# Spills by 128 partitions, tap blocks shifted by matmuls, token tiles moved by eight, weights loaded by GpSimd, and a new order, in the backward kernel of a speech encoder block

## The chip, the cores and the metric

One core of a Trainium2 chip runs the whole program. Its engines are TensorE (PE, with its weight loads as PEld), VectorE (DVE), ScalarE (ACT), GpSimd (POOL) and SyncE (SP); DMAs are issued by SP, ACT and GpSimd. The metric is the device time of one execution in microseconds, the median over runs. Lower is better.

## The reference

The block is an E-Branchformer layer: x is layer-normalized, one branch is global attention over all 4000 tokens, the other a local branch with a five-tap depthwise convolution as a gate; both are concatenated, passed through a five-tap depthwise convolution (dw_merge), projected by w_merge, and added to x. The kernel returns the output and, for a given grad_out, the gradients of all eight inputs. B = 2, T = 4000, D = 144, K = 5, bf16.

```
xa  = layernorm(x)
q, k, v = split(xa @ w_qkv)
attn = softmax(q @ k^T * D**-0.5) @ v
glob = attn @ w_att_out
h   = gelu(layernorm(x) @ w_mlp_in);  u, g = split(h);  g = layernorm(g)
gc[t] = sum_i gpad[t + i] * dw_csgu[i]              # i = 0..4
loc = (u * gc) @ w_mlp_out
m   = concat(glob, loc)
mc[t] = sum_i mpad[t + i] * dw_merge[i]
out = x + (m + mc) @ w_merge
out, vjp = jax.vjp(block, x, 7 weights)
return out, *vjp(grad_out)
```

## The kernel before

Tokens lie in tiles of 125 partitions (PB) by 32 blocks (NB) per batch, so a tensor of a batch is 125 x 32 x 144. A copy of 125 partitions is made in two DMAs, by `move` and `load_tok`: rows 0 to 111, and the 13 rows from 112.

The program has three stages that overlap at their ends.

*Head* (to about 50 us): x is loaded and normalized (xa_aug), transposed by TensorE, and the weights are loaded (`Head.loads`), transposed and multiplied into fused matrices. `Head.vu` makes, for each half h of the merge, the product VU of taps and weights, and a small block VUs of five taps by 16 rows (the last 16 of the 144 channels): GpSimd multiplies it into the tile sr (128 x 2 x 80), TensorE multiplies sr by w_merge, ACT casts the result, and it is spilled to VUs_d. What the tail needs is that block at four row offsets of 16, so the tail clears two tiles and loads VUs_d four times each, at shifted rows (lines 1632 to 1635).

*Attention* (`phase_att`): 64 steps, one for each block of 125 queries of both batches. A step computes scores S by TensorE (lines 1187 and 1194), the row minimum by DVE (L1209), the exponent by ACT (L1215), which is Pbuf, its transpose PT by two DMA transposes (L1219), and Y = P times xa by TensorE (L1236). For the gradient it computes dP the same way, multiplies it by P (ACT L1225, DVE L1226: Sbuf), transposes that by DMA (L1405: ST), multiplies it by xa (Z, L1266), and adds up the gradient of xa over the keys (X, L1322, added to acc by DVE, L1329). Beside the steps the local branch runs in units of two blocks (steps 2 to 27 for batch 0, 34 to 61 for batch 1). It goes forward and backward over a ring of neighbours, and where a batch's units go round, the last unit's tiles hgr, dugr and gpr are kept in DRAM (`keep`, stored in `e_m`, loaded by `e_hold`), as is a part of the ring (`held`). The tensors xa of batch 0 (xa_d, eight parts) and acc of batch 0 (acc_d, four parts) are spilled to DRAM in the loop and loaded again in the tail (load_xa0, load_acc0).

*Tail* (from about 1026 us): out is computed by `out_g` (TensorE L1708 and L1710, with x added by DVE, L1711), x is loaded by `load_x` in groups of four blocks, each in two DMAs, and out is stored in the same groups; dx, the weight gradients and the final products follow.

The order of instructions on each engine is written out in the code: the class `Planner` has a table `ORDER`, one list of numbers for each of PE, DVE, Activation, Pool and SP, and `plan` ties each engine's runs of instructions into that order. An engine takes its instructions in this order alone, so an instruction that waits holds back all that stand behind it on its engine, and SP's list is the order in which nearly all DMAs are issued, the transposes of PT (L1219), ST (L1405), qt (L1165) and dhT (L691) among them.

## Time and profile before

| | us |
|---|---|
| median of 3 runs | 1149.53 (1149.24 to 1152.27) |
| profiled execution | 1152.39 |
| its span on the core | 1150.5 |
| PE busy | 1118.8 (97%) |
| DVE busy | 1021.0 (89%) |
| ACT busy | 906.5 (79%) |
| POOL busy | 249.5 (22%) |

The granted clock of TensorE is 0.999 in mean. A row of a view reads "line engine operation out<-in"; SPq and POOLq are the queues on which SP and GpSimd issue DMAs, and an instruction DMA_DIRECT2D there is the issue of one DMA. The time of such an issue is that of the issuing engine; when the data have landed is another number. A row of waits reads: engine, line, what it waited for, total us, times, longest.

### The profile page before, as it was taken

The page shows a single profiled execution, that of the slowest core. Times are in us where ns is not written, and L with a number is a line of the kernel's source. Part 1 is how long each engine was busy: PE and PEld are TensorE (multiplying, and loading weights), DVE is VectorE, ACT ScalarE, POOL GpSimd, SP SyncE. Part 2 cuts the span into 40 slices and gives each one's busy share as a digit, 9 for nine tenths or more (in the row PEclk, how much of TensorE's full clock was granted, in tenths as well). Part 3 has the DMA queues.
Part 4 walks back from the last instruction along what each step waited for, and adds up shares of the span by engine and source line. Part 5 has one row for each costly group of instructions (what it writes and reads, how often), then busy time and mean ns, then how long its engine had stood idle before and what let it go on. Part 6 is the DMA issues. An engine that isn't in the chain of part 4 may idle for free.

```text
span 1150.5 us, 35851 instructions
## 1 busy us (share of the span) xinstructions
PE 1118.8 (97%) x14293; PEld 868.7 (76%) x14293; DVE 1021.0 (89%) x3063; ACT 906.5 (79%) x1641; POOL 249.5 (22%) x427
## 2 busy tenths in 40 slices
PE   6999999999999999999999999999999999999998
PEld 3667777777777677777777777777777777699987
DVE  8699999999999998877999999999999997667656
ACT  5999898899898767777989889888889877615372
POOL 8111112111121113431001111111111112013642
PEclk9999999999999999999999999999999999999999
DMA  4688887979988989998988989888888899978973
GB/s 117 155 160 176 173 181 158 192 159 173 174 166 159 188 181 182 201 187 183 207 183 178 171 158 168 161 181 152 173 174 154 187 177 183 224 173 219 245 144 101
DMA packets 680887, 200.72 MB, mean 174 GB/s; under 512 B 657815, under 2 KB 674093, under 8 KB 680699
## 3 DMA queue, kind: packets, MB, share of 16 engines
q1 hardware_dynamic: 678352, 194.69, 84.6%
q0 software_dynamic: 2192, 3.62, 1.1%
q8 instruction: 111, 1.82, 0.7%
q14 instruction: 56, 0.46, 0.1%
q10 hardware_dynamic: 176, 0.12, 0.0%
HBM read 24.62 MB, written 18.01 MB: 37 GB/s over the span
## 4 chain that ended last, share of the span: by engine, by line
PE 64%; DMA 13%; DVE 11%; ACT 7%; issue 2%; SPq 1%; POOL 1%; ACTq 0%; DVEq 0%; POOLq 0%
PE X L1322 18%; PE ps L1187 14%; PE yz L1236 8%; PE yz L1266 8%; PE ps L1194 5%; DMA PT<-Pbuf 5%; DVE Pbuf L1209 4%; ACT Pbuf L1215 3%; PE po L1708 2%; DMA ST<-Sbuf 2%; PE pd L610 1%; DVE Sbuf L1226 1%; PE pj L1147 1%; ACT Sbuf L1225 1%; DMA go_h<-in_grad_out_dram 1%
## 5 line engine op out<-in xcount | busy, mean ns | idle before, releaser
L1209 DVE TENSOR_SCALAR_CACHE_REDUCE Pbuf<-ps 125x1000 bf16<-125x1000 f32 x256 | 306.2, 1197 | 30.1 <-PE ps L1194 22.4
L1225 ACT CAST Sbuf<-ps 125x1000 bf16<-125x1000 f32 x249 | 248.7, 999 | 86.7 <-PE ps L1194 66.2
L1215 ACT ACTIVATE Pbuf<-Pbuf,nm 125x1000 bf16<-125x1000 bf16 x256 | 284.9, 1144 | 4.4 <-DVE nm L1211 4.2
L1322 PE MATMUL X<-QBs,Pbuf 125*128 125x144 bf16 x2048 | 281.1, 226 | 0.2 <-POOL QBs L1256 0.2
L1322 PE MATMUL X<-QBs,Sbuf 125*128 125x144 bf16 x2048 | 281.3, 226 | 0.0
L1187 PE MATMUL ps<-xaT_m,qt 128*128 128x500 bf16 x1024 | 260.6, 374 | 5.0 <-DVE Pbuf L1209 3.5
L1322 PEld LDWEIGHTS <-Sbuf 125*128 125x128 bf16 x2048 | 198.2, 98 | 18.8 <-issue 18.5
L1322 PEld LDWEIGHTS <-Pbuf 125*128 125x128 bf16 x2048 | 200.2, 98 | 1.3 <-issue 1.1
L1226 DVE TENSOR_TENSOR Sbuf<-Sbuf,Pbuf 125x1024 bf16<-125x1024 bf16 x249 | 170.8, 690 | 7.9 <-ACT Sbuf L1225 6.0
L1236 PE MATMUL yz<-xa_aug,PT 125*128 125x145 bf16 x2048 | 151.0, 227 | 6.5 <-DMA PT<-Pbuf 6.4
L1266 PE MATMUL yz<-xa_aug,ST 125*128 125x144 bf16 x2048 | 150.8, 228 | 3.6 <-DMA ST<-Sbuf 2.4
L1236 PEld LDWEIGHTS <-PT 125*128 125x128 bf16 x2048 | 130.7, 98 | 21.6 <-DMA PT<-Pbuf 10.5
L1187 PEld LDWEIGHTS <-qt 128*128 128x128 bf16 x1024 | 91.4, 97 | 68.6 <-issue 7.0
L1266 PEld LDWEIGHTS <-ST 125*128 125x128 bf16 x2048 | 132.9, 98 | 12.2 <-issue 7.1
L1329 DVE TENSOR_TENSOR acc<-X,acc 125x432 f32<-125x432 f32 (+1 forms) x204 | 109.8, 548 | 15.3 <-PE X L1322 14.8
L1256 POOL TENSOR_TENSOR QBs<-g,g 125x144 bf16<-125x144 f32 x64 | 35.2, 550 | 379.2 <-ACT g L1255 290.9
L1194 PEld LDWEIGHTS <-qt 16*128 16x128 bf16 x1024 | 26.3, 91 | 108.9 <-issue 108.9
L1194 PE MATMUL ps<-XR,qt 16*128 16x500 bf16 x1016 | 100.4, 380 | 0.0
L681 POOL TENSOR_SCALAR l_w<-ring,nc,c 125x144 f32<-125x144 bf16 x64 | 31.8, 504 | 167.0 <-DVE nc L677 122.4
L653 DVE TENSOR_TENSOR l_prod<-ring,Wc 125x720 bf16<-125x720 bf16 x128 | 65.9, 535 | 0.2
L1611 PE MATMUL Hps<-Yg,go_h 125*128 125x144 bf16 x640 | 54.3, 226 | 0.0
L600 POOL TENSOR_TENSOR rsr<-ve,mhalf 125x2 f32<-125x2 f32 x32 | 25.4, 795 | 126.9 <-DVE ve L599 107.4
(540 smaller groups left out, 1946.4 us busy)
## 6 DMA issues: line engine op xcount, KB each, us to landing
Yn_d<-yn SPq DMA_DIRECT2D x64, 36.0 KB
Zn_d<-qb SPq DMA_DIRECT2D x64, 36.0 KB
ug_d<-ugr SPq DMA_DIRECT2D x32, 72.0 KB
Yg<-Yn_d SPq DMA_DIRECT2D x8, 288.0 KB
Yg<-ug_d SPq DMA_DIRECT2D x8, 288.0 KB
Zn<-Zn_d SPq DMA_DIRECT2D x4, 576.0 KB
PT<-Pbuf SPq DMA_TRANSPOSE x128
ST<-Sbuf SPq DMA_TRANSPOSE x128
```

The lines of the kernel that those rows point to most:

```text
L653: nc.vector.tensor_tensor(prod[:, bi].rearrange("p a b -> p (a b)"), ring[:, a, p + bi:p + bi + 5, :].rearrange("p a b -> p (a b)"), W.Wc[ ...
L1187: mm = nc.tensor.matmul(pp[r // 2][:, r % 2, 0:CH], QT[i][:, 2 * h, :], bs(i)[0].xaT_m[:, c * CH:(c + 1) * CH], start=True, stop=False)
L1194: nc.tensor.matmul(pp[r // 2][:, r % 2, 0:CH], QT[i][rs, 2 * h + 1, :], xr, start=False, stop=True)
L1209: nc.vector.tensor_scalar(pv(pc(i, c2)), src, -1.0, 3.0e38, op0=ALU.mult, op1=ALU.min, accum_out=NM[i][:, c2:c2 + 1])
L1215: nc.scalar.activation(v, v, ACT.Exp, bias=NM[i][:, 4:5], scale=-1.0)
L1225: nc.scalar.copy(pv(sc(i, c2)), src)
L1226: nc.vector.tensor_tensor(sc(i, c2), sc(i, c2), pc(i, c2), op=ALU.mult)
L1236: nc.tensor.matmul(Yw, PT[0:PB, pos(i, j), :], S.xa_aug[:, j, 0:D + 1], start=(j == 0), stop=(j == NB - 1))
L1266: nc.tensor.matmul(Zw, ST[0:PB, j, :], S.xa_aug[:, j, 0:D], start=(j == 0), stop=(j == NB - 1))
L1322: nc.tensor.matmul(X[:, jj, :], l, r, start=(n_ == 0), stop=(n_ == len(ops) - 1))
L1329: nc.vector.tensor_tensor(av, X[0:PB, 0:nj, :], av, op=ALU.add)
L1611: nc.tensor.matmul(H[0:rows, a // 3, (a % 3) * D:(a % 3 + 1) * D], lhs, self.src[b][h][:, 2 + j, :], start=(n == 0 and a % 3 == 0), stop=( ...
```

## The change

Five parts.

1. *Weights.* Twelve loads of `Head.loads` (dw_merge, one; each half of w_merge, and w_att_out and w_mlp_out, two each; w_mlp_in, three) are issued by GpSimd and no longer by SP. w_qkv stays with ACT.
2. *Tap blocks.* sr becomes the middle of a tile of 176 columns that GpSimd clears. TensorE multiplies four windows of it by w_merge (8 matmuls of 128 x 144 for each h, before 2 of 80 x 144), ACT casts two tiles of 128 x 288 for each h (before one of 80 x 144), and VUs_d holds the four shifted blocks. The tail loads each in one DMA and clears nothing.
3. *Spills.* keep, xa_d and acc_d have 128 partitions and are moved in one DMA each. The tiles have 128 partitions too; their last rows are cleared by GpSimd (hgr, dugr, gpr, acc; acc is 4608 columns wide) or by two DMAs of SP from a zeroed tensor (xa).
4. *Tail.* `load_x` loads eight blocks at a time, and `out_g` stores eight at a time, but for the last two groups of batch 1.
5. *Order.* All five lists of `ORDER` are new. SP issues 750 DMAs and transposes in place of 826, GpSimd's list has 442 instead of 423 runs of instructions, PE's 1387 instead of 1385, ACT's 1644 instead of 1642, and DVE's as many as before.

The diff, with the lists cut to one line each of two engines:

```diff
         ld(self.Wqkv, k.w_qkv, 0)
-        ld(self.Wo, k.w_att_out, 0, nc.sync)
-        nc.sync.dma_start(self.dwt[:], k.dw_merge)
-        ld(self.Wl, k.w_mlp_out, 0, nc.sync)
-        for h in range(2):
-            ld(self.Wm[h], k.w_merge, h * D, nc.sync)
-        nc.sync.dma_start(W.Wi[0:128, 0, :], k.w_mlp_in[0:128, :])
-        nc.sync.dma_start(W.Wi[96:96 + DR, 1, :], k.w_mlp_in[128:D, :])
-        nc.sync.dma_start(self.Wi2[:], k.w_mlp_in[128:D, :])
+        e = nc.gpsimd
+        e.dma_start(self.dwt[:], k.dw_merge)
+        for h in (1, 0):
+            ld(self.Wm[h], k.w_merge, h * D, e)
+        ld(self.Wo, k.w_att_out, 0, e)
+        ld(self.Wl, k.w_mlp_out, 0, e)
+        e.dma_start(W.Wi[0:128, 0, :], k.w_mlp_in[0:128, :])
+        e.dma_start(W.Wi[96:96 + DR, 1, :], k.w_mlp_in[128:D, :])
+        e.dma_start(self.Wi2[:], k.w_mlp_in[128:D, :])
...
         W.VU.append(spill(k, v, "VU_d%d" % h))
-        sr = wt.tile([128, 2, 80], BF, name="sr%d" % h)
+        sw = wt.tile([128, 2, 176], BF, name="sr%d" % h)
+        nc.gpsimd.memset(sw[:], 0.0)
+        sr = sw[:, :, 48:128]
         for ch in range(2):
...
-        vs = wt.tile([80, D], BF, name="VUs%d" % h)
-        pt = self.ps([128, D], F32)
-        for ch in range(2):
-            nc.tensor.matmul(pt[0:80, :], sr[:, ch, :], self.Wm[h][:, ch, :], start=(ch == 0), stop=(ch == 1))
-        nc.scalar.copy(vs[:], pt[0:80, :])
+        vs = wt.tile([128, 4, D], BF, name="VUs%d" % h)
+        for q in range(2):
+            pt = self.ps([128, 2, D], F32)
+            for p in range(2):
+                a = 48 - DR * (2 * q + p)
+                for ch in range(2):
+                    nc.tensor.matmul(pt[:, p, :], sw[:, ch, a:a + 128], self.Wm[h][:, ch, :], start=(ch == 0), stop=(ch == 1))
+            nc.scalar.copy(vs[:, 2 * q:2 * q + 2, :], pt[:])
         W.VUs.append(spill(k, vs, "VUs_d%d" % h))
...
     nc.gpsimd.dma_start(held[1][PB - 1:PB].rearrange("p a b c -> p (a b c)"), k.zdram[0:1, 0:4 * D])
-    keep = [tc.dram_tile([PB, G2, n], BF, name="keep%d_%d" % (b, i)) for i, n in enumerate((D, D, 2 * D))]
+    keep = [tc.dram_tile([128, G2, n], BF, name="keep%d_%d" % (b, i)) for i, n in enumerate((D, D, 2 * D))]
     prod = pl.tile([PB, G2, 5, D], BF, name="l_prod")
...
         nc.gpsimd.memset(t[96:128], 0.0)
-    hgr = mk("hgr", [PB, G2, 2 * D], 3)
-    dugr = mk("dugr", [PB, G2, D], 3)
-    gpr = mk("gpr", [PB, G2, 2 * D], 3)
+    def whole(name, n):
+        full = mk(name, [128, G2, n], 3)
+        nc.gpsimd.memset(full[2][96:128], 0.0)
+        return full, [t[0:PB] for t in full]
+    hgf, hgr = whole("hgr", 2 * D)
+    dugf, dugr = whole("dugr", D)
+    gpf, gpr = whole("gpr", 2 * D)
     rsr = mk("rsr", [PB, 2 * G2], 4, F32)
...
     def e_hold():
...
             move(nc.sync, ring[:, :, 8 + 2 * i:10 + 2 * i, :], held[i])
-        move(nc.sync, hgr[0][:, :, 0:D], keep[0][:])
-        move(nc.sync, dugr[0][:], keep[1][:])
-        move(nc.sync, gpr[0][:], keep[2][:])
+        nc.sync.dma_start(hgf[0][:, :, 0:D], keep[0][:])
+        nc.sync.dma_start(dugf[0][:], keep[1][:])
+        nc.sync.dma_start(gpf[0][:], keep[2][:])
...
     def e_m(g):
...
         if g == NG2 - 1:
-            move(nc.sync, keep[0][:], hgr[new(g)][:, :, 0:D])
-            move(nc.sync, keep[1][:], dugr[new(g)][:])
-            move(nc.sync, keep[2][:], gpr[new(g)][:])
+            nc.sync.dma_start(keep[0][:], hgf[new(g)][:, :, 0:D])
+            nc.sync.dma_start(keep[1][:], dugf[new(g)][:])
+            nc.sync.dma_start(keep[2][:], gpf[new(g)][:])
...
 class Planner:
...
-        "Pool": [8, 5, 15, 4, 11, 0, 12, 10, 1, 3, 47, 7, 2, 16, 18, 6, 19, 17, 41, 25, 26, 24, 50, 33, 32, 31, 9, 53, 37, 38, 20, 30, 42, 23, 13,
...
-        "SP": [0, 1, 4, 3, 19, 2, 30, 5, 6, 9, 16, 21, 44, 10, 7, 45, 13, 18, 27, 39, 22, 46, 40, 60, 14, 12, 15, 23, 11, 8, 25, 31, 26, 28, 32, 20,
...
+        "Pool": [0, 22, 27, 7, 4, 2, 14, 1, 10, 9, 8, 20, 28, 19, 31, 30, 11, 6, 23, 29, 53, 37, 38, 36, 13, 44, 43, 45, 49, 12, 50, 32, 21, 15, 39,
...
+        "SP": [0, 1, 3, 2, 5, 4, 18, 48, 27, 13, 11, 6, 7, 30, 34, 29, 9, 15, 49, 10, 19, 20, 8, 21, 22, 24, 23, 26, 17, 14, 16, 12, 25, 35, 42, 31,
...
     def __init__(self, tc, nc):
...
         for h in range(2):
-            k.nc.gpsimd.memset(self.VUs[h][:], 0.0)
-            for a in range(4):
-                k.nc.sync.dma_start(self.VUs[h][DR * a:DR * a + 80, a, :], self.W.VUs[h][:])
+            k.nc.sync.dma_start(self.VUs[h][:], self.W.VUs[h][:])
...
         S = self.SS[0]
-        S.acc = m0.tile([PB, NB, D], F32, name="acc0")
-        S.xa_aug = m0.tile([PB, NB, XW], BF, name="xa0r")
+        self.acc0, self.xa0 = m0.tile([128, NB, D], F32, name="acc0"), m0.tile([128, NB, XW], BF, name="xa0r")
+        S.acc, S.xa_aug = self.acc0[0:PB], self.xa0[0:PB]
...
     def load_xa0(self):
...
             sl = slice(16 * g, 16 * g + 16)
-            move(k.nc.sync, S.xa_aug[:, sl, 0:D], k.xa_d[:, sl, :])
+            k.nc.sync.dma_start(self.xa0[:, sl, 0:D], k.xa_d[:, sl, :])
...
     def load_acc0(self):
...
             sl = slice(8 * g, 8 * g + 8)
-            move(k.nc.sync, S.acc[:, sl, :], k.acc_d[:, sl, :])
+            k.nc.sync.dma_start(self.acc0[:, sl, :], k.acc_d[:, sl, :])
...
     def load_x(self, b, g):
-        b0 = GB * g
-        xo = self.wk.tile([PB, GB, D], BF, tag="xo", bufs=9)
-        move(self.k.nc.sync, xo, tok_view(self.k.x, b)[:, b0:b0 + GB, :])
-        return xo
+        if g % 2 == 0:
+            b0 = GB * g
+            self.xo = self.wk.tile([PB, 2 * GB, D], BF, tag="xo", bufs=4)
+            move(self.k.nc.sync, self.xo, tok_view(self.k.x, b)[:, b0:b0 + 2 * GB, :])
+        return self.xo
...
     def out_g(self, b, g, xo):
...
-            nc.vector.tensor_tensor(xo[:, 2 * p2:2 * p2 + 2, :], po[:], xo[:, 2 * p2:2 * p2 + 2, :], op=ALU.add)
-        move(nc.sync, tok_view(k.out0, b)[:, b0:b0 + GB, :], xo)
+            o = GB * (g % 2) + 2 * p2
+            nc.vector.tensor_tensor(xo[:, o:o + 2, :], po[:], xo[:, o:o + 2, :], op=ALU.add)
+        if b == 1 and g >= k.NG - 2:
+            o = GB * (g % 2)
+            move(nc.sync, tok_view(k.out0, b)[:, b0:b0 + GB, :], xo[:, o:o + GB, :])
+        elif g % 2:
+            move(nc.sync, tok_view(k.out0, b)[:, b0 - GB:b0 + GB, :], xo)
...
     bx = pool(ctx, "bx", "left")
-    acc = bx.tile([PB, NB, D], F32, name="acc")
+    accf = bx.tile([128, NB, D], F32, name="acc")
+    acc = accf[0:PB]
     rstd = [bx.tile([PB, NB], F32, name="rstd_x%d" % b) for b in range(B)]
...
             setattr(S, nm + "_d", tc.dram_tile([128, NB, D], BF, name="%s_d%d" % (nm, b)))
-    k.acc_d = tc.dram_tile([PB, NB, D], F32, name="acc_d")
-    k.xa_d = tc.dram_tile([PB, NB, D], BF, name="xa_d")
+    k.acc_d = tc.dram_tile([128, NB, D], F32, name="acc_d")
+    k.xa_d = tc.dram_tile([128, NB, D], BF, name="xa_d")
...
     def open_batch(b, side):
...
         px = pool(es_x[b], "xa%d" % b, side)
-        S.xa_aug = px.tile([PB, NB, XW], BF, name="xa_aug%d" % b)
+        S.xa_full = px.tile([128, NB, XW], BF, name="xa_aug%d" % b)
+        S.xa_aug = S.xa_full[0:PB]
         pa = pool(es_x[b], "bt%d" % b, side)
...
     k.close_batch0 = es_x[0].close
-    k.spill_xa0 = lambda j: move(nc.sync, k.xa_d[:, j:j + 4, :], SS[0].xa_aug[:, j:j + 4, 0:D])
-    k.spill_acc0 = lambda sl: move(nc.sync, k.acc_d[:, sl, :], acc[:, sl, :])
+    k.spill_xa0 = lambda j: nc.sync.dma_start(k.xa_d[:, j:j + 4, :], SS[0].xa_full[:, j:j + 4, 0:D])
+    k.spill_acc0 = lambda sl: nc.sync.dma_start(k.acc_d[:, sl, :], accf[:, sl, :])
     A = K()
...
     def clear_a():
+        nc.gpsimd.memset(accf[96:128], 0.0)
+        for a, n in ((0, 25), (25, 7)):
+            nc.sync.dma_start(SS[0].xa_full[PB:128, a:a + n, :].rearrange("p a b -> p (a b)"), k.zdram[0:128 - PB, 0:n * XW])
         nc.gpsimd.memset(A.dWiT[:], 0.0)
```

GpSimd in the head, up to the first rstd (L374 before, L380 after: the first power of the normalization of x). Before:

```order
L138 MEMSET M1T 128x144
L295 MEMSET WiT 128x144
L2014 MEMSET xa_aug_114 125x32
L136 MEMSET two 128x7x144
L374 TENSOR_TENSOR rstd_x_65<-lnve_100,mhalf 125x8
```

After:

```order
L157 DMA dwt<-in_dw_merge_dram 5x288
L140 MEMSET RW 128x432
L136 MEMSET two 128x7x144
L153 DMA raw<-in_w_mlp_out_dram 128x144
L28 ISA
L28 AFFINE_SELECT ident<-ident 128x128
L153 DMA raw<-in_w_merge_dram 128x144
L154 DMA raw<-in_w_merge_dram 16x144
L153 DMA raw<-in_w_merge_dram 128x144
L64 MEMSET go_q_95 32x576
L380 TENSOR_TENSOR rstd_x_65<-lnve_100,mhalf 125x8
```

Five loads of weights now stand ahead of the first rstd, dw_merge first; three clears moved behind it.

GpSimd around the products sr of the tap blocks (L282 before, L285 after). Before:

```order
L240 TENSOR_SCALAR sWm_310<-raw,cols 128x144 x2
L1132 MEMSET yn_133 32x144
L282 TENSOR_TENSOR sr_806<-two,cols 128x80
L282 TENSOR_TENSOR sr_834<-two,cols 128x80
L244 COPY sWr_312<-sWm_310 128x2x5x16
L282 TENSOR_TENSOR sr_834<-two,cols 128x80
L282 TENSOR_TENSOR sr_806<-two,cols 128x80
L402 COPY go_r_96<-go_q_95 125x608
```

After:

```order
L138 MEMSET M1T 128x144
L1139 MEMSET qb_130 128x768
L285 TENSOR_TENSOR sr_806<-two,cols 128x80
L1141 MEMSET yn_133 32x144
L2038 MEMSET acc 32x4608
L285 TENSOR_TENSOR sr_806<-two,cols 128x80
L310 COPY Wc<-Wc 128x5x144
L285 TENSOR_TENSOR sr_843<-two,cols 128x80
L164 DMA Wi_197<-in_w_mlp_in_dram 16x288
L285 TENSOR_TENSOR sr_843<-two,cols 128x80
```

The clear of acc's last rows and a weight load now stand between the products of the two tap blocks, and other clears ahead of them.

SP where batch 0's kept rows come back (`e_hold`; PT and ST are the transposes of Pbuf and Sbuf). Before:

```order
L1219 DMA_TRANSPOSE PT<-Pbuf 128x16x128 x2
L48 DMA hgr_934<-keep_0_926 13x2x144
L1165 DMA_TRANSPOSE qt<-qb_128 128x6x128
L691 DMA_TRANSPOSE dhT<-dhr_948 128x6x128
L48 DMA dugr_937<-keep_1_927 13x288
L662 DMA ug_d_70<-ugr_931 128x288
L1405 DMA_TRANSPOSE ST<-Sbuf 128x16x128
L662 DMA ug_d_70<-ugr_930 128x288
L1405 DMA_TRANSPOSE ST<-Sbuf 128x16x128
L691 DMA_TRANSPOSE dhT<-dhr_947 128x6x128
L47 DMA dugr_937<-keep_1_927 112x288
L1219 DMA_TRANSPOSE PT<-Pbuf 128x16x128 x2
```

After:

```order
L1228 DMA_TRANSPOSE PT<-Pbuf 128x16x128
L1280 DMA Zn_d_71<-qb_128 128x144
L1228 DMA_TRANSPOSE PT<-Pbuf 128x16x128
L645 DMA dugr_959<-keep_1_948 128x288
L1257 DMA Yn_d_69<-yn_132 128x144
L1174 DMA_TRANSPOSE qt<-qb_128 128x6x128
L1414 DMA_TRANSPOSE ST<-Sbuf 128x16x128
L701 DMA_TRANSPOSE dhT<-dhr_972 128x6x128
L47 DMA ring<-held_1_945 112x2x288
L1414 DMA_TRANSPOSE ST<-Sbuf 128x16x128
L1280 DMA Zn_d_71<-qb_130 128x144
L1280 DMA Zn_d_71<-qb_129 128x144
```

Where two halves of a kept tile (112 and 13 rows) were issued on both sides of transposes, one load of 128 rows stands, and stores of Zn and Yn have moved among the transposes.

More of the change, by code (lines that the diff above doesn't have):

```diff
@@ L778 @@
     ORDER = {
[53 rows of a table removed]
-        "DVE": [0, 2, 1, 3, 4, 10, 5, 11, 9, 8, 6, 7, 12, 14, 15, 13, 16, 17, 40, 43, 25, 18, 44, 20, 22, 23, 19, 32, 24, 21, 34, 33, 35, 36, 26, 28,
[102 rows of a table removed]
-        "Activation": [1, 0, 4, 5, 2, 3, 7, 6, 8, 9, 10, 13, 29, 32, 14, 15, 11, 33, 16, 17, 18, 12, 37, 35, 34, 19, 20, 21, 24, 22, 23, 31, 27, 26,
[64 rows of a table removed]
-        "Pool": [8, 5, 15, 4, 11, 0, 12, 10, 1, 3, 47, 7, 2, 16, 18, 6, 19, 17, 41, 25, 26, 24, 50, 33, 32, 31, 9, 53, 37, 38, 20, 30, 42, 23, 13,
[44 rows of a table removed]
[54 rows of a table added]
+        "DVE": [1, 0, 2, 3, 4, 11, 5, 9, 8, 7, 6, 10, 23, 12, 14, 15, 24, 16, 13, 17, 42, 22, 19, 21, 18, 40, 25, 44, 43, 32, 20, 34, 26, 28, 33, 35,
[102 rows of a table added]
+        "Activation": [1, 0, 4, 5, 2, 3, 6, 7, 8, 9, 10, 13, 14, 29, 15, 11, 18, 16, 37, 17, 35, 30, 33, 23, 12, 19, 20, 24, 21, 36, 26, 27, 22, 25,
[64 rows of a table added]
+        "Pool": [0, 22, 27, 7, 4, 2, 14, 1, 10, 9, 8, 20, 28, 19, 31, 30, 11, 6, 23, 29, 53, 37, 38, 36, 13, 44, 43, 45, 49, 12, 50, 32, 21, 15, 39,
[42 rows of a table added]
     }
```

523 rows, old and new, of the table ORDER are left out of this document.

## The prediction

> **What bounds the kernel now.** I read the page's busy times first, then a table by stage, then the waits of TensorE, then the chain. The page:
>
> ```profile
> PE 1118.8 (97%) x14293; PEld 868.7 (76%) x14293; DVE 1021.0 (89%) x3063; ACT 906.5 (79%) x1641; POOL 249.5 (22%) x427
> ```
>
> TensorE has 1118.8 us of work in a span of 1150.5, so only 31.7 us can go unless its work shrinks. The table by stage (window, its length, busy time of PE, PEld, DVE, ACT and POOL, granted clock, DMA share, GB/s) says where they lie:
>
> ```profile
> 0.00:17.00 17.00, 8.60 (x53) 5.49 (x54) 13.60 (x64) 7.50 (x23) 12.35 (x26) 1.00 0.63 163
> 17.00:50.00 33.00, 31.05 (x313) 20.05 (x313) 21.89 (x51) 28.79 (x70) 14.35 (x33) 1.00 0.40 100
> 50.00:110.00 60.00, 57.30 (x655) 41.15 (x653) 56.27 (x154) 56.59 (x109) 8.02 (x13) 1.00 0.85 176
> 110.00:365.00 255.00, 254.48 (x3229) 194.97 (x3228) 249.53 (x747) 226.68 (x408) 42.85 (x66) 1.00 0.88 173
> 365.00:445.00 80.00, 74.88 (x950) 55.13 (x948) 73.73 (x228) 57.67 (x100) 14.29 (x24) 1.00 0.93 180
> 445.00:880.00 435.00, 431.11 (x5379) 326.89 (x5377) 402.35 (x1146) 372.75 (x651) 82.14 (x142) 1.00 0.90 176
> 880.00:1005.00 125.00, 121.62 (x1539) 91.33 (x1538) 106.90 (x288) 91.80 (x151) 18.70 (x34) 1.00 0.99 187
> 1005.00:1026.00 21.00, 21.00 (x326) 20.13 (x324) 11.25 (x23) 5.31 (x10) 1.44 (x3) 1.00 0.90 208
> 1026.00:1110.00 84.00, 82.27 (x1333) 80.76 (x1331) 60.68 (x263) 42.37 (x77) 42.15 (x72) 1.00 0.90 207
> 1110.00:1147.00 37.00, 36.53 (x542) 32.77 (x539) 24.75 (x105) 17.08 (x53) 13.25 (x18) 1.00 0.38 105
> ```
>
> Window less PE busy is TensorE's idle time: 8.4 us before 17, 1.95 up to 50, 2.7 in 50 to 110, 0.5 in 110 to 365, 5.1 in 365 to 445, 3.9 in 445 to 880, 3.4 in 880 to 1005, none in 1005 to 1026, 1.7 and 0.5 in the tail, and the last 3.5 us have no PE at all. The loop (50 to 1005) holds 15.6 of them. Its densest losses are where the local unit of a batch starts again from held rows (365 to 445, 880 to 1005) and where the first units start (50 to 110). TensorE's waits name the releasers; first the whole span, then the windows 365:445 (two rows), 880:1005 and 50:110 (one each):
>
> ```profile
> PE yz L1236 <- DMA PT<-Pbuf: 6.4, 11, 1.0
> PE hps L170 <- DMA raw<-in_w_qkv_dram: 6.3, 1, 6.3
> ...
> PE hps L215 <- DMA dwt<-in_dw_merge_dram: 1.4, 1, 1.4
> ```
>
> ```profile
> PE yz L1236 <- DMA PT<-Pbuf: 1.7, 3, 0.9
> PE yz L1266 <- DMA ST<-Sbuf: 1.2, 1, 1.2
> ```
>
> ```profile
> PE yz L1236 <- DMA PT<-Pbuf: 2.4, 3, 1.0
> ```
>
> ```profile
> PE yz L1266 <- DMA ST<-Sbuf: 0.8, 1, 0.8
> ```
>
> In those three places TensorE waits 1.7 + 1.2 + 2.4 + 0.8 = 6.1 us for the transposes that SP issues. That is what a shorter SP queue can reach.
>
> **The weights by GpSimd.** Twelve loads leave SP. The chain's pieces (start, length, what) and one timeline row of DVE:
>
> ```profile
> 7.43 3.08 DMA dwt<-in_dw_merge_dram
> ...
> 11.05 0.95 PE pt L392 x8
> ```
>
> ```profile
> 9.53 1.05 DVE L385 TENSOR_SCALAR xa_aug<-Sbuf,rstd_x,lnnm 125x144 bf16<-125x144 bf16 x4
> ```
>
> dwt is the wait of 1.4 us above, and lands at 10.51. In the new order it is GpSimd's first load, ten rows ahead of the first rstd, and may land at once. But the transposes of L392 that come next need xa_aug, normalized until 9.53 + 1.05 = 10.58; they begin at 11.05. The gain ends there: between 0 and 0.47, taken -0.35. The wait of 6.3 for w_qkv is on ACT's queue and stays.
>
> GpSimd pays for the issues. Rows of it in the head and the tail, then the landing time of its stores:
>
> ```profile
> 20.98 0.74 POOL L535 DMA_DIRECT2D held<-zdram  x1
> ...
> 42.07 0.33 POOL L548 MEMSET ugr<- 32x288 bf16 x1 [11.26 <-PE pt L350]
> 42.46 0.46 POOL L2023 MEMSET A_dWiT<- 128x432 f32 x1
> ```
>
> ```profile
> 1069.25 0.50 POOL L106 DMA_DIRECT2D XR<-in_w_qkv_dram  x1
> ```
>
> ```profile
> out_dram<-dxo POOLq DMA_DIRECT2D x16, 126.0 KB, 2.7
> ```
>
> An issue costs 0.50 to 0.74, nearer 0.50 for weights (the row of w_qkv): 12 x 0.55 = 6.6 us. The cleared rows of acc are 4608 wide; by 0.46 for 432 that is 4.9. At that rate two clears of the tap blocks (352 wide) add 0.7; the held load (0.74) and one clear of 240 columns (0.3) now come later. 6.6 + 4.9 + 0.7 - 0.74 - 0.3 = +11.2. GpSimd was done at 42.07 - 11.26 = 30.81, so it ends the same work at about 42.0. What waits for it is the tap block's first product, on TensorE at 45.4 (row below). So I cost this at nothing, by a cover of 3.4 us; by the other end, 0.74 an issue, it is 44.3 and 1.1 us are left. If the cover goes, TensorE stalls there one for one. The clears of the padded rows of hgr, gpr and dugr come behind and are small.
>
> One thing could break that cover: GpSimd's issues might wait for DVE. DVE is busy 13.60 of the first 17 us and the held load at 20.98, beside a DVE 66% busy, took 0.74, which is the dearer end above and not a multiple of it. The Trainium skill, page "SBUF — State Buffer", section "A bandwidth-pool intuition that's wrong (but worth ruling out)", says that a DMA issued by GpSimd which takes about 620 ns alone can take about 3100 ns beside a VectorE copy, since GpSimd cannot write descriptors meanwhile. By that figure twelve would be 37 us instead of 6.6, an estimate of about 1177 us for the kernel; the row of 0.74 does not agree with it, and I keep 0.55.
>
> **The tap block by TensorE.** Per head, 2 matmuls become 8, and one cast of 80 x 144 becomes two of 128 x 288. Rows of line L286, its piece of the chain, and the nearest cast of ACT:
>
> ```profile
> L286 PE MATMUL hps<-raw,sr x4: 226/226/226, 45.4 to 47.1; 128*80 128x144 bf16 x4
> ```
>
> ```profile
> 45.59 0.12 PE hps L286 x2
> ```
>
> ```profile
> L260 ACT CAST VUT<-hps x5: 387/397/412, 30.9 to 33.1; 128x288 bf16<-128x288 f32 x5
> ```
>
> The chain passes two matmuls in 0.12 us, so twelve more cost 12 x 0.06 = +0.7, since TensorE is dense there. Four casts at 0.40 in place of two small ones are +1.0 on ACT; between 42 and 54 the chain runs on TensorE, so they are beside it (0 to +1.0). Taken for both: +0.7. In the tail two loads take the place of eight: six issues of SP, counted with the others of the tail below.
>
> **Spills by 128 rows.** Six moves per batch for the kept rows, eight of xa_d and four of acc_d lose their second issue: 24 in all. Rows of L48, the 13-row half (min/median/max in ns), the slowest and quickest of the kept ones among them, and one such issue in the chain:
>
> ```profile
> L48 SPq DMA_DIRECT2D xa_d<-xa_aug x8: 369/520/547, 27.4 to 510.5; - x8
> ```
>
> ```profile
> L48 SPq DMA_DIRECT2D acc_d<-acc x4: 338/460/1199, 536.1 to 589.0; - x4
> ```
>
> ```profile
> L48 SPq DMA_DIRECT2D hgr<-keep x2: 863/865/867, 378.7 to 908.2; - x2
> L48 SPq DMA_DIRECT2D dugr<-keep x2: 343/415/487, 383.5 to 901.0; - x2
> ```
>
> ```profile
> 397.70 0.42 SPq L47
> ```
>
> 8 x 0.52 + 4 x 0.46 + 12 x 0.64 (the middle of the last two rows) = 13.7 us of SP's time, against 6.1 us of TensorE's waits that they can touch. Much lies at 110 to 365 or 445 to 880, where TensorE hardly waits, and saves nothing. Near the held rows an issue ahead of a transpose delays it directly, as the chain's piece at 397.70 shows. But a transpose also waits for the exponent and for DVE's product, which no SP issue shortens, so I take 55% of 6.1: -3.4, between 0 and -6.1. The upper end is not zero: the order now puts the 128-row loads of kept rows between transposes at other places, and a wait it adds could be as large as those it removes, +6.1. Two loads that clear xa's pads come in the head, ahead of the spreads of R to XR; I take 0, and +0.7 (two issues) as their upper end.
>
> **Loads and stores of eight tiles.** 30 issues fewer, with six fewer for xa0 and acc0. One load's and one store's row:
>
> ```profile
> L47 SPq DMA_DIRECT2D xo<-in_x_dram x16: 317/341/1347, 1031.7 to 1121.8; - x16
> L47 SPq DMA_DIRECT2D out_dram<-xo x16: 317/354/533, 1059.2 to 1147.1; - x16
> ```
>
> With the six of the tap blocks 42 x 0.35 = 15 us of SP, but TensorE idles only 1.7 + 0.5 = 2.2 us in that stage, and some of this waits for ACT and DVE. Taken -0.9, between 0 and -2.2; a first x group twice as large lands later by 126 KB at the stage's 207 GB/s, +0.6 at worst. The last stores keep their size, so the 3.5 us behind the last matmul stay.
>
> **The order besides.** Other moves are small swaps on every engine. TensorE's remaining idle time in the loop is 15.6 - 6.1 = 9.5. Bounds -9.5 and +9.5; no row prices a swap, so the middle, 0.
>
> **Sum.** -0.35 + 0.7 - 3.4 - 0.9 = -3.95, say -4.0. The profiled execution took 1152.39 (span 1150.5 and 1.9 around it), 2.9 above the median of 1149.53; against it the sum gives 1148.4, and against the median 1145.5, which I predict. A measurement of this kernel can tell about 0.3%, 3.4 us, from no change.
>
> **Rivals.**
> - The order repays most of what is left. For it: the longest of TensorE's waits for PT is 1.0 us, and an order written out for every engine can shift waits of that size. Against: 110 to 365 already has 0.5 us only. Two thirds of 15.6, with the other terms, give 1149.5 - 10.4 - 0.55 = 1138.6, 1138 to 1141.
> - All is hidden, or waits move one place on. For it: 97% busy, and each engine near its limit where the waits are (DVE 92% in 365 to 445). The extra matmuls and the head then cancel: 1149.5, 1147.5 to 1151.5.
> - GpSimd is late at the tap block. Its cover of 3.4 us is gone when an issue takes 0.83 us; at 1.1 to 1.5 TensorE stalls 3.2 to 8 and, with nothing won elsewhere, gives 1153 to 1158. Against: the rows of 0.50 to 0.74.
> - GpSimd's issues go on only while DVE rests. DVE rests 3.4 + 11.1 of the first 50 us, 29%, so an issue of 0.55 becomes 1.9; twelve cost 16 us more, 13 beyond the cover: 1162. Against: the same rows. The Trainium skill's section named above would have it so for VectorE's copies; no row here does.
> - The order makes new waits. PE and SP both follow a fixed order, and each of 128 transposes of PT holds SP for 1.7 us:
>
> ```profile
> L1219 SPq DMA_TRANSPOSE PT<-Pbuf x128: 1547/1698/3760, 30.7 to 1009.6; - x128
> ```
>
>   One put behind a load that waits for its kept row stops Y or Z. If the 6.1 us double and nothing is won: about 1155.5. It decides from 3.4 us of new waits.
>
> **How the numbers follow.** The forecast 0.45, with its own range 1142.5 to 1148.5, of which 0.28 lies below 1146.1 (faster) and 0.17 within 0.3%. Order repays: 0.18, faster. Hidden: 0.20, same. GpSimd late: 0.05 (0.04 slower). GpSimd behind DVE: 0.02, slower. New waits: 0.10 (0.09 slower). Faster 0.46, same 0.39, slower 0.15. The range 1139.5 to 1152.5 leaves out the slower ones (0.15) and the lower part of the second (0.05).
>
> **What the changed profile would show.** Right: no wait of L215 for dwt; L392 within 0.5 us of before; the tap block's matmuls starting without a wait for GpSimd; PE idle in 365 to 445 and 880 to 1005 down from 8.5 to about 5; 750 SP issues; the tail's PE idle near 1.3. Wrong: GpSimd issues above 0.83 us in the head, a new row "PE ... <- POOL sr", larger totals for PT or ST, or idle time at places that were dense (110 to 365). A gain there or in 445 to 880 beyond 2 us would mean that the order, not the issues, decided.

## The result and the profile after

The changed kernel takes 1162.15 us (median of 4 runs, 1159.68 to 1164.26), the kernel before in the same runs 1150.75 (1149.24 to 1152.27). The ratio is 1.0097 with a 95% interval of 1.0078 to 1.0115: 11.4 us slower, where 1145.5 was predicted and the range ended at 1152.5. The profiled execution has a span of 1162.0. Its busy times, then the table by stage in windows as shown for before, and the end (length, busy PE, PEld, DVE, ACT, POOL, granted clock, DMA share, GB/s):

```profile
PE 1122.9 (97%) x14305; PEld 873.1 (75%) x14305; DVE 1018.3 (88%) x3063; ACT 908.5 (78%) x1643; POOL 261.7 (23%) x446
```

```profile
365.00:445.00 80.00, 74.52 (x920) 54.69 (x919) 71.10 (x212) 56.28 (x97) 13.81 (x23) 0.98 0.90 175
445.00:880.00 435.00, 427.63 (x5353) 325.54 (x5351) 398.68 (x1135) 368.95 (x644) 83.35 (x143) 1.00 0.88 176
880.00:1005.00 125.00, 122.86 (x1551) 92.05 (x1548) 108.62 (x309) 93.19 (x154) 17.89 (x33) 1.00 0.94 187
...
1026.00:1110.00 84.00, 79.38 (x1261) 78.92 (x1259) 56.38 (x244) 37.73 (x69) 37.76 (x66) 0.98 0.85 200
...
1147.00:1162.00 15.00, 9.55 (x138) 8.56 (x136) 5.47 (x23) 1.65 (x8) 4.64 (x6) 0.96 0.27 73
```

TensorE has 4 us more of busy time in a span 11.5 us longer; the larger part of the loss is idle time. It is 7.4 us in 445 to 880 (3.9 before) and 4.6 in 1026 to 1110 (1.7 before). In 365 to 445 it is 5.5, as before (5.1), but the granted clock there is 0.98 and fewer matmuls were done (920 against 950), so that window hides a loss. Following the same matmuls through both traces gives the places: level at the first Y (-0.5 us), +0.3 at step 12 of the 64 steps, +1.1 at step 21, +4.8 at step 23, +6.3 at step 36, +5.4 at step 60, then in the tail +5.9 at 1074 us and +10.0 at the last output matmuls. The rest is behind the last matmul: it ends 5.4 us before the end of the span, in before 3.9 (at 1146.53; the prediction counted 3.5, from the edge of its last window). TensorE's waits over the whole span:

```profile
PE yz L1245 <- DMA PT<-Pbuf: 6.0, 6, 3.1
PE pm L1543 <- DVE xo L1720: 4.4, 2, 2.8
...
PE yz L1275 <- DMA ST<-Sbuf: 3.3, 5, 1.6
```

The wait for dwt is gone, as forecast. PT costs as much as before (6.0 against 6.4) in fewer, longer waits: one of 3.1, where the longest was 1.0. The second row is new.

**The jump at step 23.** Here batch 0's local units go round, and `e_hold` loads the kept rows. First TensorE's timeline in the changed kernel, then ScalarE's row of the last exponents of the step's first half, then SP's issues:

```profile
396.30 0.55 PE L1331 MATMUL X<-WiT,dhT 128*128 128x144 bf16 x6
399.99 2.13 PE L1245 MATMUL yz<-xa_aug,PT 125*128 125x145 bf16 x16 [3.14 <-DMA PT<-Pbuf]
401.91 1.53 PE L1196 MATMUL ps<-xaT_m,qt 128*128 128x500 bf16 x4
...
403.69 1.19 PE L1245 MATMUL yz<-xa_aug,PT 125*128 125x145 bf16 x16
```

```profile
389.88 1.14 ACT L1224 ACTIVATE Pbuf<-Pbuf,nm 125x1000 bf16<-125x1000 bf16 x1
```

```profile
390.87 0.38 SPq L646 DMA_DIRECT2D gpr<-keep  x1
391.29 2.30 SPq L701 DMA_TRANSPOSE dhT<-dhr  x1
393.64 0.58 SPq L672 DMA_DIRECT2D ug_d<-ugr  x1
394.26 0.60 SPq L644 DMA_DIRECT2D hgr<-keep  x1
394.96 0.89 SPq L48 DMA_DIRECT2D ring<-held  x1
395.98 3.86 SPq L1228 DMA_TRANSPOSE PT<-Pbuf  x2
```

The first half of Pbuf is done at 389.88 + 1.14 = 391.0. Its transpose is issued at 395.98, behind five other issues, three of them loads of kept rows. In before both transposes of PT stood there as one row, with the loads of kept rows ahead of it and behind it:

```profile
390.53 5.77 SPq L1219 DMA_TRANSPOSE PT<-Pbuf  x2
```

TensorE runs dry at 396.85 and stands until 399.99. Then it is slow as well: the same 16 matmuls take 2.13 us, and 1.19 at 403.69. The granted clock (the column behind the busy times) says why:

```profile
400.00:402.00 2.00, 2.00 (x17) 2.00 (x18) 0.00 (x0) 0.00 (x0) 0.27 (x1) 0.50 0.93 211
402.00:404.00 2.00, 2.00 (x14) 0.78 (x13) 0.20 (x1) 0.16 (x1) 0.00 (x0) 0.76 0.86 195
```

A wait of 3.1 us so costs about 4.5: 0.9 more for the 16 matmuls (401.91 - 399.99 against the 1.02 that they advance at full clock) and 0.5 for the scores behind them. The Trainium skill, page "TensorE: Matmul & The Clock Gate", section "Part 1: The HAM clock gate (the "warmup" mystery)", has the clock fall to half after an idle window of about 3.4 us; in this trace 3.14 us were enough.

**The jump in the tail.** Waits of the changed kernel from 1085 to 1112, then one wait of before from 1050 to 1112, then GpSimd's rows in the changed kernel and in before:

```profile
DVE t L1747 <- POOL dxo L1750: 9.1, 3, 6.0
...
POOL dxo L1750 <- DMA out_dram<-dxo: 6.9, 2, 4.4
...
PE pm L1543 <- DVE xo L1720: 4.4, 2, 2.8
```

```profile
POOL dxo L1737 <- DMA out_dram<-dxo: 6.0, 2, 5.0
```

```profile
1082.81 1.27 POOL L1750 TENSOR_TENSOR dxo<-t,go_h 125x576 bf16<-125x576 f32 x1 [2.69 <-issue]
1086.66 1.28 POOL L1750 TENSOR_TENSOR dxo<-t,go_h 125x576 bf16<-125x576 f32 x1 [2.58 <-DMA out_dram<-dxo]
...
1088.95 0.53 POOL L48 DMA_DIRECT2D out_dram<-dxo  x1
...
1096.06 1.27 POOL L1750 TENSOR_TENSOR dxo<-t,go_h 125x576 bf16<-125x576 f32 x1 [4.37 <-DMA out_dram<-dxo]
```

```profile
1087.47 1.27 POOL L1737 TENSOR_TENSOR dxo<-t,go_h 125x576 bf16<-125x576 f32 x1 [3.75 <-ACT t L1735]
1089.04 0.53 POOL L48 DMA_DIRECT2D out_dram<-dxo  x1 [0.29 <-POOL dxo L1737]
```

The chain reads upwards from TensorE: the transposes of pm wait for DVE's xo (which frees their place), DVE stands up to 6.0 us at t until GpSimd has summed an older t into dxo, and GpSimd waits for an older store of dxo to land. GpSimd's waits for its stores are not new: 6.9 us against 6.0 in before. Nor do the stores land later: from 1050 to 1140 the 126 KB ones take 2.7 us in the changed kernel and 4.5 in before, from issue to landing (medians). What differs at this place is when a store is issued. The sum that is done at 1082.81 + 1.27 = 1084.08 is stored from 1088.95 on, 4.9 us later, behind a second sum and two loads of weights; in before the store's first issue follows 0.3 us behind its sum (at 1089.04). That GpSimd's order makes the stall is read from the trace; the runs below don't show it.

### The profile page after: what moved, and what is told of

Same layout as the page of the kernel before. It is cut to its first block, busy times and chain, and to the rows that moved or that the text cites. A ratio compares the mean times of both kernels' runs of the same rounds, so it can differ in the third digit from the quotient of the medians.

```text
span 1162.0 us, 35810 instructions
## 1 busy us (share of the span) xinstructions
PE 1122.9 (97%) x14305; PEld 873.1 (75%) x14305; DVE 1018.3 (88%) x3063; ACT 908.5 (78%) x1643; POOL 261.7 (23%) x446
```

## The experiments

Theory A: the new order makes new waits, and the edits themselves cost little. Theory B: the edits cost it. "Old order" is the table of before, where a new instruction stands beside its neighbour; a mixed order is one table up to a program point and the other behind it. Each time stands against the kernel before in the same runs. Times are from those comparisons; profiles give the places only, since two profiles of equal head code (runs 9 and 15) differed by 2.2 us at the first Y.

**1. All edits, old order.**

```diff
-    ORDER = {...}   # the new table
+    ORDER = {...}   # the table of before
```

> All edits of the change, with the order of before: every instruction that both kernels have stands where it stood, a 128-row spill where its 112-row half stood, a load or store of eight tiles where that of its first (load) or last (store) four tiles stood, GpSimd's weight loads at their new places. Theory A (the new order makes the new waits: a transpose of PT held behind other issues at 390 to 396 us, stores of dx held together in the tail) expects a ratio to before of 0.996 to 1.000: the edits alone save up to 4 us. Theory B (the edits themselves cost it: larger DMAs in the tail that slow others, GpSimd's issues) expects 1.008 to 1.010, as the changed kernel.

1154.77 against 1152.85, ratio 1.0014 (0.9997 to 1.0031). The same edits that lose 0.97% in the new order lose 0.14% in the old one: 0.0083 x 1150 = 9.5 us hang on the table. Theory A holds for most of the loss; by the two intervals the 9.5 could be 3 more or less.

**2. The code of before, new order.**

```diff
-    ORDER = {...}   # the table of before
+    ORDER = {...}   # the new table
```

> The code of before without any edit, in the new order: each instruction that both have stands where the new order has it, both halves of a spill side by side at the place of the one DMA, groups of four tiles in pairs, SP's twelve weight loads behind the loads of x. Theory A (order) expects a ratio of 1.008 to 1.015, since the issues are also more. Theory B (edits) expects 0.998 to 1.002.

1187.01, ratio 1.0293 (1.0268 to 1.0319). That is more than either theory expected. The first Y is 11.6 us late, with the weights on SP again (TensorE waits 4.3 for w_att_out and 3.5 for dw_merge). The kernel is 33 us behind at step 63, and 38 at the last matmul, so the loop loses 22 and the tail 5. A table fits one set of instructions: its worth can't be measured with another, so this run says nothing about the size in the changed kernel.

**3. New order up to step 60, old behind it (edits kept).**

```diff
     ORDER = {...}   # the new table up to step 60
+                    # behind it the sequence of before
```

> All edits and the new order up to attention step 60, the order of before from there on. Theory A expects the tail's 5 to 6 us back: a ratio of 1.004 to 1.006, with the delay of 4 us at step 23 and 1.5 at step 35 left. Theory B expects 1.008 to 1.010.

1157.15, ratio 1.0042 (1.0027 to 1.0056): the tail's order is worth 0.0055, 6 us. TensorE in the tail of this run:

```profile
1026.00:1110.00 84.00, 82.66 (x1351) 81.78 (x1349) 60.24 (x251) 39.55 (x72) 38.96 (x67) 1.00 0.79 209
1110.00:1147.00 37.00, 37.00 (x551) 33.40 (x549) 26.67 (x114) 19.73 (x57) 15.78 (x22) 1.00 0.41 116
```

It idles 1.3 us there, against 5.6 in the changed kernel (84 - 79.38 and 0.95 in the second window), with the same loads and stores of eight.

**4. Six SP issues of step 23 put in another order.**

```diff
-    gpr<-keep  dhT  ug_d<-ugr  hgr<-keep  ring<-held  PT  PT
+    gpr<-keep  PT  dhT  ug_d<-ugr  PT  hgr<-keep  ring<-held
```

> The changed kernel with six issues of SP swapped at one place, where batch 0's kept rows are loaded: the two transposes of PT of step 23 stand ahead of dhT and of the loads of hgr and ring, not behind them. Theory A (SP's order at this place) expects TensorE's wait of 3.1 us for PT at 397 to 400 and the slow clock behind it to be gone, so 3 to 5 us less than the changed kernel: a ratio to before of 1.005 to 1.007. Rival (the stall comes from the traffic of the 128-row loads and moves one step on): no change, 1.008 to 1.010.

1157.68, ratio 1.0052 (1.0033 to 1.0071), so 0.0045 or 5 us from one place on one queue. SP's issue of PT there, and what TensorE still waits for in 375 to 415:

```profile
391.78 3.54 SPq L1223 DMA_TRANSPOSE PT<-Pbuf  x1
```

```profile
PE yz L1240 <- DMA PT<-Pbuf: 1.8, 2, 1.4
PE ps L1191 <- DMA qt<-qb: 1.5, 1, 1.5
```

PT now goes out at 391.78 instead of 395.98. The wait for PT shrinks, and the next one, for qt, appears behind it. The profiled execution is this run's slowest (1162.45): it is 2.9 us ahead of the changed kernel's at step 27 and 0.8 at the last matmul. So the 5 us rest on the times; the profile shows the gain at this place and its loss further on.

**5 and 6. The new order for the head only; and both cures together.** Run 5 keeps the edits, with the new table up to step 2 and the old one behind it. Run 6 is run 4 with the old tail of run 3.

```diff
     ORDER = {...}   # run 5: the new table up to step 2
+                    # behind it the sequence of before
     ORDER = {...}   # run 6: the new table with PT ahead at step 23, up to step 60
+                    # behind it the sequence of before
```

> All edits; the new order up to attention step 2, the order of before from there to the end. With the old order throughout, the edits stood 3 to 4 us late at the first steps (GpSimd's weight loads in an order not made for them) and were level at the end. If the edits save what the prediction said once their head fits (spills -3.4, tail -0.9, tap blocks +0.7, head -0.35), the ratio to before is 0.996 to 0.999. If the edits save nothing and only the head costs or pays, it is 0.999 to 1.002.

> The changed kernel with both cures: PT of step 23 ahead on SP, and the order of before from step 60 on. If the two losses are separate places and add up, 1.0097 - 0.0045 - 0.0055 gives a ratio of 0.9985 to 1.001. If one cure only lets another wait come up, 1.003 to 1.005.

Run 5: 1150.44 against 1150.45, ratio 0.9997 (0.9986 to 1.0008). With the new order in the head alone, all four edits together cost nothing. The 0.0017 to run 1 lie within the two intervals, so that the head needed the new order is likely, not shown. Run 6: 1155.24, ratio 1.0043 (1.0021 to 1.0065), no better than either cure alone. The two don't add up, and about 5 us are left that neither place explains. By the profiles, run 6 is 3.7 us ahead of run 3 at step 60 and 0.6 at the last matmul: what the swap frees is lost again in the tail. One wait there, which run 3 hasn't got, is 1.9 us for xa0r, a load of spilled rows:

```profile
PE pz L1683 <- DMA xa0r<-xa_d: 1.9, 1, 1.9
```

**7 and 8. The old tail for one queue alone.**

```diff
-        "SP": [...]     # run 7: the new tail
+        "SP": [...]     # the old tail
-        "Pool": [...]   # run 8: the new tail
+        "Pool": [...]   # the old tail
```

> The changed kernel, in which SP alone takes the order of before from step 60 on; the other four engines keep the new one. If SP's bunched loads (about 2 MB issued in 4 us at 1074 to 1079) delay the stores of dx, GpSimd no longer waits 4 us for them and most of the tail's 5 to 6 us come back: 1.004 to 1.007. If GpSimd's own order holds the stores, nothing comes back: 1.008 to 1.011.

> The changed kernel, in which GpSimd alone takes the order of before from step 60 on. If GpSimd's own order (four issues of stores and two of weights in a row behind two sums dxo) makes the stall, 1.004 to 1.007. If it is SP's loads, 1.008 to 1.011.

1178.59, ratio 1.0238 (1.0215 to 1.0262), and 1168.4, ratio 1.0155 (1.0133 to 1.0178): both slower than the changed kernel, which neither expectation had. New waits of TensorE come up in their tails, the longest 9.6 us for DVE's xo (run 7) and 4.5 for GpSimd's go_r (run 8). So the 6 us of the tail come back when all engines change order together, and from neither of these two lists alone; whether SP's loads or GpSimd's order hold the stores of dx stays open.

**9. The spills by 128 rows alone, old order.**

```diff
-        move(nc.sync, dugr[0][:], keep[1][:])
+        nc.sync.dma_start(dugf[0][:], keep[1][:])
...
+        nc.gpsimd.memset(accf[96:128], 0.0)
```

> The kernel before, in its own order, with the spills by 128 rows alone (kept rows, xa_d, acc_d, and their loads in the tail; the pads' clears by GpSimd and SP where they fit). The prediction's term says -3.4 us, between 0 and -6.1: a ratio of 0.995 to 1.000, at 0.997. The rival (a 128-row DMA saves an issue but a transpose waits for other things) expects 0.999 to 1.001.

1144.97 against 1149.23, ratio 0.9961 (0.9944 to 0.9978), -4.5 us: faster than both kernels. TensorE's waits over the whole span, and the two windows of the kept rows:

```profile
PE yz L1234 <- DMA PT<-Pbuf: 2.8, 6, 0.7
```

```profile
365.00:445.00 80.00, 76.67 (x985) 57.50 (x985) 75.49 (x236) 58.09 (x99) 15.79 (x25) 1.00 0.88 182
880.00:1005.00 125.00, 123.40 (x1575) 93.62 (x1572) 105.94 (x284) 89.89 (x144) 18.08 (x33) 1.00 1.00 197
```

The waits for PT fall from 6.4 to 2.8, and the idle time of the two windows from 8.5 to 4.9. Not all of that is the edit's. The profile of before is of an execution 2.9 us above its median (1152.39), the profile here is of one 1.2 below its median (1143.81), and run 13 below, whose loop is that of before in code and order, has this:

```profile
PE yz L1230 <- DMA PT<-Pbuf: 3.8, 9, 0.6
```

```profile
365.00:445.00 80.00, 75.63 (x964) 56.06 (x963) 74.01 (x231) 57.35 (x98) 14.26 (x24) 1.00 0.92 182
880.00:1005.00 125.00, 123.01 (x1565) 92.90 (x1562) 106.62 (x285) 92.30 (x147) 17.42 (x32) 1.00 1.01 193
```

With an unchanged loop, runs 10, 11, 13 and 14 wait 3.8 to 6.0 us for PT and idle 6.2 to 8.6 us in the two windows. So about 1 us of either fall is clear of what executions differ by, and the profiles show only part of the 4.5 us at the named waits.

**10 and 13. Loads and stores of eight tiles alone, old order.** In run 10 the store of batch 1's second last group (group 6, two issues of four tiles) stands on SP ahead of stores of weight gradients, and that of the last group (7) among them. Run 13 moves group 6's behind the first dWk store, and also group 7's to the end, which the expectation doesn't name.

```diff
     out<-xo(8 tiles)  dwmo
-    xo(group 6) x2  dWv  dWq  dwmo  xo(8)  xo(group 7)  o  dWx  dWo  dwmo  xo(8)  xo(group 7)  dWo  dWk  dwmo  dWk  dWq
+    dWv  dWq  dwmo  xo(8)  o  dWx  dWo  dwmo  xo(8)  dWo  dWk  xo(group 6) x2  dwmo  dWk  dWq  xo(group 7) x2
     o
```

> The kernel before, in its own order, with loads of x and stores of out by eight tiles alone; a pair is loaded where its first group was (some later, behind the store that frees its buffer) and stored where its second was. The prediction's term says -0.9 us at most -2.2: 0.998 to 1.000. If groups twice as large come late to DVE's additions, 1.000 to 1.003.

> Before with x loaded and out stored by eight tiles, as in the run of the eights alone, with one place of SP's order changed: the store of the second last group of batch 1 (two issues of four tiles each) stands seventeen issues later, behind the first dWk store. Theory A (places in the order cost the time, the edit itself does not): SP no longer stands still from 1134 to 1143.7, its last store is issued within 1 us of before's 1148.06, and the time is 1147 to 1151, a ratio of 0.998 to 1.001. Theory B (larger transfers themselves cost): the time stays near the run before, +4 to +6, a ratio of 1.0035 to 1.005.

Run 10: 1155.68, ratio 1.0051 (1.0032 to 1.0070), +5.9 us. In its profile the last matmul is level with before (-0.4 us); the loss lies behind it. What SP waits for in 1120 to 1150, and its issues:

```profile
SPq L47 <- DVE xo L1707: 9.6, 1, 9.6
```

```profile
1143.74 0.32 SPq L47 DMA_DIRECT2D out_dram<-xo  x1
...
1152.13 0.27 SPq L1946 DMA_DIRECT2D out_dram<-o  x1
```

One store waits 9.6 us for its sum, with everything else of SP behind it, and the last issue leaves at 1152.13 (1148.06 before). With the stores moved, run 13 takes 1150.6 against 1149.3, ratio 1.0009 (0.9997 to 1.0020); its SP has no such stand:

```profile
1144.11 0.27 SPq L1946 DMA_DIRECT2D out_dram<-o  x1
```

So transfers twice as large cost most likely +1.0 us, which is not clear of zero, and the places of the two stores cost the other 5. That it is group 6's is read from SP's stand.

**11. The tap block by TensorE alone, old order.**

```diff
-        pt = self.ps([128, D], F32)
+        for q in range(2):
+            pt = self.ps([128, 2, D], F32)
+            for p in range(2):
```

> The kernel before, in its own order, with the tap blocks by TensorE alone, twelve more matmuls and two casts more in the head, six issues less in the tail. The prediction's term says +0.7 us: 1.000 to 1.001.

1152.21, ratio 1.0031 (1.0014 to 1.0047), +3.6 us. TensorE's rows of the block:

```profile
45.48 0.41 PE L291 MATMUL hps<-raw,sr 128*128 128x144 bf16 x4
46.38 0.41 PE L291 MATMUL hps<-raw,sr 128*128 128x144 bf16 x4 [0.49 <-ACT VUs L292]
...
48.08 0.81 PE L291 MATMUL hps<-raw,sr 128*128 128x144 bf16 x8
48.73 0.59 PE L1187 MATMUL ps<-xaT_m,qt 128*128 128x500 bf16 x2
```

Eight of them pass in 48.73 - 48.08 = 0.65, 0.08 each, and the first head waits 0.49 for a cast. Sixteen at 0.08 less the old four (0.26) and with the wait are +1.5; the trace is +1.7 from step 3 to 15. The remaining 2 us of the timed ratio have no place in this one profile, and stay open.

**12. New order up to step 12, old behind it (edits kept).**

```diff
     ORDER = {...}   # the new table up to step 12
+                    # behind it the sequence of before
```

> All edits; the new order up to attention step 12, the order of before from there on. In the run that changed orders at step 2, the seam itself cost about 3 us at step 4 (a transpose of PT), and the steps behind gained 5.8 us on before up to step 63. At step 12 the changed kernel stands 0.3 us behind before and little differs between the orders. If the seam was the cost, 0.995 to 0.998, faster than both kernels. If the gain behind it was only the seam's loss won back, 0.999 to 1.002.

1149.38 against 1149.23, ratio 0.9996 (0.9982 to 1.0011): as run 5. Up to step 12 the new table costs nothing, which agrees with +0.3 us at that step in the changed kernel.

**14. The weights by GpSimd alone, old order.**

```diff
-        nc.sync.dma_start(self.dwt[:], k.dw_merge)
+        e = nc.gpsimd
+        e.dma_start(self.dwt[:], k.dw_merge)
```

> Before with the twelve weight loads of the head issued by GpSimd and nothing else changed, every other instruction in its old place. Theory A (the edit needs its own head order): GpSimd's products and rstd come later by the issues ahead of them, the first Y ends 2 to 4 us later, some of it is made up in the loop, ratio 1.001 to 1.003. Theory B (the loads by GpSimd are free under the cover of 3.4 us): first Y level, ratio 0.999 to 1.001. My prediction's rival with 1.9 us an issue would give the first Y 13 us late and a ratio of 1.011.

1152.68 against 1149.3, ratio 1.0030 (1.0017 to 1.0043), +3.4 us. TensorE's waits in the first 60 us:

```profile
PE pt L393 <- ACT xa_aug L384: 1.3, 1, 1.3
PE pt L393 <- POOL xa_aug L388: 1.2, 2, 0.7
```

Here the loads stand in the old clears' company ahead of GpSimd's first rstd, which starts at 9.39 instead of 6.85. The transposes of xa_aug wait for it, and the first Y is 2.7 us late. Run 1, with the loads at the same places, agrees: 9.38, and 3.3 late. In the changed kernel the clears have moved behind it, and that rstd starts at 7.56.

**15. Spills and eights (with the store of run 13), old order.**

```diff
-        move(nc.sync, dugr[0][:], keep[1][:])
+        nc.sync.dma_start(dugf[0][:], keep[1][:])
-        move(self.k.nc.sync, xo, tok_view(self.k.x, b)[:, b0:b0 + GB, :])
+        move(self.k.nc.sync, self.xo, tok_view(self.k.x, b)[:, b0:b0 + 2 * GB, :])
```

> Before with the spills by 128 rows and the loads and stores by eight (with the store moved as in e13), old order otherwise. Theory A: the spills' -4.5 us stays and the eights add -1 to +1, so 1144 to 1146.5, a ratio of 0.995 to 0.997. Theory B: the eights cost 4 to 6 of themselves and the ratio is 0.999 to 1.002.

1148.8 against 1149.3, ratio 1.0003 (0.9987 to 1.0019). By theory A -4.5 + 1.0 = -3.5 was due; the result fits neither that nor a cost of the eights by themselves, which run 13 denies. Gains don't add up here either, and why is open. Up to the loads of the tail every engine does the same work in the same order as in run 9. Yet the profile is 2.2 us behind run 9's at the first Y and 3.7 at the end of the loop, and only 1.0 more is lost in the tail. So most of the difference lies where the two kernels are alike, and this run, whose loop has the same spills, doesn't repeat run 9's gain. Run 9 stays the fastest measured.

## Why the prediction was wrong, and where it was right

**"The order besides", taken as 0: this step failed.** I gave it bounds of -9.5 to +9.5 and took the middle, because no row of before prices a swap. Run 1 and the changed kernel put it at +9.5. That this equals the upper bound is chance: the bound was TensorE's idle time in the loop, and in the trace 5.4 of the 10.0 us at the last matmul are lost up to step 60 and 4.6 behind it. Two places are shown by changing them: SP's issues at step 23 (run 4, 5 us) and the engines' tables in the tail (run 3, 6 us). They don't add up; with both changed 5 us are left (run 6), whose place isn't shown. Step 35, where 1.5 to 2 us are lost beside a wait of 1.6 for ST, was only read from the trace, not tried. The mechanism was in my text, as the rival "the order makes new waits", with 0.10: a PT put behind a load of kept rows. It was in my excerpt of SP's order too, with the loads of keep and held among the transposes, and the error was to call such moves "small swaps" with a mean of zero. In a stage where TensorE idles 5 of 80 us a queue can gain little and lose much, so the middle of the bounds was not the likeliest value. The figure of that rival, 1155.5, was too small as well, since it doubled the 6.1 us of waits in the loop and had nothing for the tail. That another rival, "GpSimd's issues go on only while DVE rests", gave 1162 is chance; its mechanism is refuted below. I also let a wait cost its own length; the one of 3.1 us cost the clock as well and became 4.5.

**Spills: right in the run alone, the place shown in part.** -3.4 forecast, -4.5 measured alone (run 9, -6.4 to -2.5). The waits named did fall (PT 6.4 to 2.8, idle time in the two windows from 8.5 to 4.9, "about 5" in the text), but about 1 us of it is clear of what unchanged loops differ by, and run 15 doesn't repeat the gain. In the changed kernel the order of the same loads spent it again: 7.6 there (80 - 74.52 and 125 - 122.86).

**Loads and stores of eight: no gain.** -0.9 forecast, +1.0 alone (run 13, -0.3 to +2.3). Fewer issues freed an SP for which TensorE waited only 0.5 us in that stage (for Zn). The 2.2 us of idle time that I wanted to reach were misread too: 0.5 of them lie behind the last matmul, which ends at 1146.53. The end behind it, which I said would stay, is 5.4 us instead of 3.9, and run 10 with 8.2 shows that the place of two stores can put 4 us there.

**The tap block: mis-sized.** +0.7 forecast, +1.5 by rows and +3.6 timed in the old order (run 11). The step of 0.06 per matmul came from a pair with 80 columns of weights; eight with 128 columns pass at 0.08. "The casts are beside it" failed by one wait of 0.49; in the changed kernel no wait stands there.

**Weights by GpSimd: right for the changed kernel, for a reason I only half gave.** The issues and the clear of acc's rows, and the last product that the tap block needs:

```profile
4.57 0.56 POOL L153 DMA_DIRECT2D raw<-in_w_merge_dram  x1
...
33.79 3.93 POOL L2038 MEMSET acc<- 32x4608 f32 x1
...
39.63 0.33 POOL L285 TENSOR_TENSOR sr<-two,cols 128x80 bf16<-128x80 bf16 x1
```

An issue takes 0.49 to 0.66 (0.55 forecast), the clear 3.93 (4.9), the end is 39.96 (42.0), nothing waits for it, and the wait for dwt is gone. The first Y is 0.5 us earlier (0.35 forecast), which is less than profiles of equal head code differ by. The rivals "GpSimd late" and "GpSimd behind DVE" are both refuted: DVE is busy 14.22 of the first 17 us and the issue at 4.57 takes 0.56. The Trainium skill's 3100 ns beside a VectorE copy (page "SBUF — State Buffer", section "A bandwidth-pool intuition that's wrong (but worth ruling out)") don't show in these issues; the work of DVE beside the one at 4.57 is BATCH_NORM_STATS2, so a copy isn't tested. But I looked for the cover only at the tap block. Run 14 shows the nearer one: GpSimd's first rstd, which the new order guards and the old one doesn't (+3.4 us).

**The sum.** One by one in the old order the edits are -4.5, +1.0, +3.6 and +3.4, together +3.5; all at once measure +1.6 (run 1), which is no contradiction at intervals of 1 to 2 us each. With a head order that fits them they are 0 (run 5). The predicted -4.0 would have needed the order to be free and the spills alone to count.

## What to carry to other kernels

Where every engine follows a written order, price the order before the edits: at each place where the bound engine waits for a queue, list what now stands ahead of the issue it needs, and when each of those can leave. A queue in order stands at one early store or load until its data are there (9.6 us of SP in run 10, about 5 of the kernel), and here such costs had no mean of zero. Take a bundle apart: a part that gains alone (0.9961) can be worth more than all of it, and neither gains nor cures may be added without a run of both. And compare a view of the profile with that of other runs of the same code before its fall is put down to an edit: waits for PT were 3.8 to 6.4 us with the loop unchanged.

## What the runs showed of the hardware

- A wait of TensorE of 3.14 us brought the granted clock to 0.50 in the 2 us behind it and 0.76 in the next 2. In 1100 to 1105, behind waits of 2.80 and 1.64 in the tail, it was 0.77:

```profile
1100.00:1105.00 5.00, 3.18 (x33) 3.10 (x33) 5.00 (x22) 2.68 (x5) 2.35 (x5) 0.77 0.72 220
```

- Stores of dx took 1.7 to 8.0 us from issue to landing in the changed kernel and 1.7 to 7.6 in before, 2.9 in the median of both, so within one execution the landing time varies more than fourfold.
- Two executions of the same work in the same order (runs 9 and 15, up to the tail) are 2.2 us apart at the first Y and 3.7 at the end of the loop.
